# A cross-attention and maxout kernel: wider idle matmuls, two loads split in two, and a late copy of the states

## The chip, the cores and the metric

The kernel runs on one core of one Trainium2 chip. A core has five engines that run side by side, each through its own list of instructions in order: TensorE (PE in the profile, with its weight loads shown apart as PEld), VectorE (DVE), ScalarE (ACT), GpSimd (POOL) and SyncE (SP), which here issues nearly all the DMAs. An engine waits for another only through semaphores. TensorE writes to PSUM, whose banks hold 128 x 512 fp32 values; DVE and ACT copy from there to SBUF.

The metric is the device time of one execution in microseconds, and the number compared is the median over runs. Before the change it is 148.07 us, the median of 5 runs between 147.75 and 148.35.

## The reference, cut to what matters

```python
def _attn_ref(x, state):              # x: 8 x 8 x 512 x 64, state: 8 x 8 x 32 x 64
    scores = scale * x @ state.T;  a = softmax(scores);   xread = a @ state
    scores2 = scale * state @ x.T; a2 = softmax(scores2); sread = a2 @ x
    return concatenate([xread, sread], axis=2)

def _moe_ref(x, w1, w2, w_out):       # 4352 rows of 512 -> 1024 -> 512
    return np.maximum(x @ w1, x @ w2) @ w_out
```

For each batch and head, 512 rows of x read from 32 rows of state and the other way round. The result goes, token by token, through two matrices W1 and W2 of 512 x 1024, an elementwise maximum, and W_out (Wo in the code) of 1024 x 512.

## The kernel before

The kernel never forms `xread`. Since `xread = a @ state`, it multiplies the states of a batch into the weights first (`sw_mm`, tile `sw`) and then the attention weights `a` by that product. The maximum is rewritten: max(h1, h2) = h2 + relu(h1 - h2). So the first layer needs only W1 - W2 (tile `wd`, made by `w_sub`), followed by a relu into tile `r` (`l1_mm`, `l1_ev`), and the part h2 @ Wo becomes one product W2 @ Wo (tile `wwo`), made once from transposed W2 (`w2_tr_mm`, `w2t`) in `w_wo_mm`. The second layer adds up `a @ (state W2 Wo)` and `r @ Wo` in one PSUM bank for each of the four 128-row chunks of a batch (`l2_open`, `l2_f`, `l2_out`).

The order of all instructions is written out by hand. There are two parts. Lines 587 to 855 are the prologue: it loads batches 0 to 3, the states and the weights, the weights in four quarters, and interleaves the work of batch 0 with the making of `wd` and `wwo`, quarter by quarter, as they arrive. It ends with the first layer of batch 1. Lines 858 to 894 are a loop over the batches from 1 on: second layer of batch b, with the scores, the softmax and the `sw` product of batch b + 1 between its chunks. So the second layer of batch 1 (`b == 1`) is the first thing in the loop, and the scores of batch 2 come just ahead of it.

TensorE has its own fillers: `idle(n)` issues n matmuls of zeros, 256 columns wide, into a bank that nobody reads. There are 32 of them: 15 at the start, and groups of one, three and four between the first steps of batch 0.

The states. The block-diagonal tile `sbd` holds the transposed states of all batches; its zeros are written once. The states of batches 0 and 1 go through TensorE. Those of batches 2 to 7 are loaded together (`sfr`), cast on POOL (`sbr`), and transposed by one DMA into the tile `stt` (`states_dma`). `states_ev(1, "A")` and `states_ev(0, "V")` (lines 829 and 831) then copy one half each of `stt` into `sbd`, on ACT and on DVE. They stand ahead of the first relus of batch 1 in the lists of both engines. `scores_mm` (line 262) reads `sbd` for its batch, and so does `sw_mm`.

PSUM is two pools of four banks, `ps` and `pa`. The eight first-layer products of batch 1 alternate between them, and the two small transposes behind them, `sread_tr_mm(1, pa)` and `sread_tr_mm(0, pa)` (lines 846 and 850, L353 in the profile), take the `pa` banks that the relus of steps 6 and 5 on ACT have emptied.

The first attention weights. `norm_mul_pair(0, 2, "P")` and `norm_mul_pair(0, 3, "V")` (lines 668 and 669) multiply the exponentials by the reciprocal sums for head pairs 2 and 3 of batch 0, on POOL and DVE; `at_mm` transposes the result.

The DMAs of SP go out in the order of the code. There are eight completion semaphores for them, taken in turn, so that a DMA is issued only when the one eight places earlier has landed; besides, a load into a buffer waits until that buffer's last reader is done.

Of the kernel before, what the change touches and what calls it, by code (L numbers as in the profile page):

```python
# [8 lines left out]
F32 = mybir.dt.float32  # L9
# [6 lines left out]
def kernel(  # L16
# [9 lines left out]
    nc = tc.nc  # L26
    B, H, S, D = x.shape
    _, _, Ns, _ = state.shape
    L = S + Ns
    DM = H * D  # L30
    FF = moe_w1.shape[1]
    NC = S // 128
    NF = FF // 128
    NQ = 4
    FQ = FF // NQ
# [5 lines left out]
    stage = ctx.enter_context(tc.tile_pool(name="stage", bufs=1))  # L41
# [5 lines left out]
    pa = ctx.enter_context(tc.tile_pool(name="pa", bufs=4, space=bass.MemoryType.PSUM))  # L47
    ctx.enter_context(tc.manual_schedule())

    def bank(dtype=F32, pool=None):  # L50
        n = 512 if dtype == F32 else 1024
        if pool is pa:
            return pa.tile([128, n], dtype, tag="acc", name="acc")
        return ps.tile([128, n], dtype, tag="ps", name="ps")

    def copy(eng, o, i):
        if eng == "A":
            nc.scalar.copy(o, i)  # L58
        elif eng == "V":
            nc.vector.tensor_copy(o, i)  # L60
        else:
            nc.gpsimd.tensor_copy(o, i)  # L62
# [4 lines left out]
    wz = consts.tile([128, 512], BF16, name="wz")  # L67
    sbd = consts.tile([128, B, 4, 2 * Ns], BF16, name="sbd")
    wd = consts.tile([128, 4, FF], BF16, name="wd")
    wwo = consts.tile([128, 4, DM], BF16, name="wwo")  # L70
    wo = consts.tile([128, NF, DM], BF16, name="wo")
# [11 lines left out]
    xf_t, st = {}, {}  # L83
# [12 lines left out]
    w2f, w1f, wof, w2b = {}, {}, {}, {}  # L96

    def load_w2(q, second=False):
        wf, w, tag = (w1f, moe_w1, "w1f") if second else (w2f, moe_w2, "w2f")
        wf[q] = stage.tile([128, 4, FQ], F32, tag=tag, bufs=3, name=tag)  # L100
        nc.sync.dma_start(out=wf[q], in_=w[:, q * FQ:(q + 1) * FQ].rearrange("(i p) f -> p i f", p=128))

    def load_w1(q):
        load_w2(q, True)

    def load_wo(q):
        wof[q] = stage.tile([128, 2, DM], F32, tag="wof", bufs=3, name="wof")
        nc.sync.dma_start(out=wof[q], in_=moe_w_out[q * FQ:(q + 1) * FQ, :].rearrange("(f p) n -> p f n", p=128))  # L108
# [15 lines left out]
    P = {}  # L124
# [35 lines left out]
        P["st"] = xio.tile([128, NC * 256], BF16, tag="xb", name="stt")  # L160
        nc.sync.dma_start_transpose(out=P["st"].rearrange("p (m r) -> p m r", m=8), in_=sbr.rearrange("p m j d -> p (m j d)"))

    def states_ev(j, eng):
        o = sbd[64 * j:64 * j + 64, 2:B, :, 32 * j:32 * j + 32].rearrange("p b k (l m) -> p (b k) l m", l=4)
        copy(eng, o, P["st"][64 * j:64 * j + 64, :].rearrange("p (m k l) -> p k l m", m=8, l=4)[:, 8:])


    def cast_half(b, g, eng):
# [5 lines left out]
    def cast_x(b, engs):  # L174
        for g in range(2):
            cast_half(b, g, engs[g])
# [11 lines left out]
    def cast_pair(b, k, eng, m=1):  # L188
        xo = st[b]["xo"]
        for j in range(k, k + m):  # L190
            copy(eng, xo[:, :, j, 2:130].rearrange("p c (i d) -> p i c d", i=2),
                 xf_t[b][:, 2 * j:2 * j + 2, :].rearrange("p i (c d) -> p i c d", c=NC))

    def xt_pair_mm(b, k, pool=None):
        d = st[b]
        if "xt" not in d:
            d["xt"] = at.tile([128, NC, 4, 128], BF16, tag="xt", name="xt")
        p = P["xt", k] = bank(BF16, pool)
        for c in range(NC):
            nc.tensor.transpose(p[:, c * 128:(c + 1) * 128], d["xo"][:, c, k, 2:130], ident)  # L200

    def xt_pair_ev(b, k, eng):
        copy(eng, st[b]["xt"][:, :, k, :], P["xt", k][:, 0:512].rearrange("p (c t) -> p c t", c=NC))

    def att_tiles(b):
        d = st[b]
        d["e"] = at.tile([128, 2, NC, 4, Ns], BF16, tag="e", name="e")
        d["a"] = at.tile([128, 2, NC, 4, Ns], BF16, tag="a", name="a")
        d["es"] = at.tile([128, 2, 2 * NC, 2], F32, tag="es", name="es")
        d["er"] = at.tile([128, 2, 2 * NC, 2], F32, tag="er", name="er")  # L210

    def scores_pair_mm(b, k, pool):
        d = st[b]
        if "e" not in d:
            att_tiles(b)
        p = P["sc", k] = bank(F32, pool)
        for c in range(NC):
            nc.tensor.matmul(p[:, c * 64:c * 64 + 64], d["xt"][:, c, k, :], sbd[:, b, k, :],
                             start=(c == 0), stop=(c == NC - 1))
# [74 lines left out]
        (nc.gpsimd if eng == "P" else nc.vector).tensor_mul(  # L294
            av, ev, d["er"][:, hh].unsqueeze(3).to_broadcast([128, 2 * NC, 2, Ns]))

    def norm_mul_pair(b, k, eng):
        d = st[b]
        ev = d["e"].rearrange("p g c i n -> p (g c) i n")[:, :, k, :]
        av = d["a"].rearrange("p g c i n -> p (g c) i n")[:, :, k, :]  # L300
        (nc.gpsimd if eng == "P" else nc.vector).tensor_mul(
            av, ev, d["er"][:, k // 2, :, k % 2].unsqueeze(2).to_broadcast([128, 2 * NC, Ns]))

    def norm(b, hh, eng, sums=True):
        norm_sums(b, hh, sums)
# [137 lines left out]
    def l2_open(b, c, p, start, stop):  # L443
        for g in range(2):
            nc.tensor.matmul(p, AT[b][:, g, c, :], SW[b][:, g, FF:WC], start=(start and g == 0), stop=(stop and g == 1))  # L445

    def l2_f(b, c, p, fs, start, stop):
        for j, f in enumerate(fs):
            nc.tensor.matmul(p, R[b][:, f, c * 128:(c + 1) * 128], wo[:, f, :],  # L449
                             start=(start and j == 0), stop=(stop and j == len(fs) - 1))  # L450

    def l2_out(b, c, p, eng):
        if b not in OB:
            OB[b] = big.tile([128, NC, DM], F32, tag="ob", name="ob")
        copy(eng, OB[b][:, c, :], p)

    def l2(b, c):
        p = bank(F32, pa)
        l2_open(b, c, p, True, False)
        l2_f(b, c, p, range(NF), False, True)  # L460
        l2_out(b, c, p, "A" if c % 2 else "V")
# [56 lines left out]
    def w1_cast_h(j, eng):  # L518
        copy(eng, w1b[:, :, 128 * j:128 * j + 128], w1f[0][:, :, 128 * j:128 * j + 128])

    def wo_cast_h(j, eng):
        copy(eng, wo[:, j, :], wof[0][:, j, :])
# [23 lines left out]
    def w_sub(q, i0, i1, eng):  # L546
        (nc.gpsimd if eng == "P" else nc.vector).tensor_sub(  # L547
            wd[:, i0:i1, q * FQ:(q + 1) * FQ], w1f[q][:, i0:i1], w2f[q][:, i0:i1])

    def wo_cast(q, eng):  # L550
        copy(eng, wo[:, 2 * q:2 * q + 2, :], wof[q])

    ROUNDS = [[0], [1], [2], [3]]

    def w_wo_mm(r, i, pool=None):
        p = P["wwo", r, i] = bank(F32, pool)
        fs = [f for q in ROUNDS[r] for f in (2 * q, 2 * q + 1)]
        for f in fs:
# [7 lines left out]
    def w_wo_ev(r, i, eng):  # L566
        if r == 0:
            copy(eng, w2acc[:, i, :], P["wwo", r, i])
        else:
            nc.vector.tensor_tensor(wwo[:, i, :] if r == len(ROUNDS) - 1 else w2acc[:, i, :], P["wwo", r, i],  # L570
                                    w2acc[:, i, :], op=ALU.add)

    idle_p = [None]

    def idle(n, cols=256):
        if idle_p[0] is None:
            idle_p[0] = bank(F32, pa)
        for j in range(n):
            nc.tensor.matmul(idle_p[0][:, 0:cols], wz[:, 0:128], wz[:, 0:cols], start=True, stop=True)  # L579

    def l2_part(q, c):
        if ACC[c] is None:
# [14 lines left out]
    load_h(1, 0)  # L597
    load_state(1, nc.sync)
    load_w2(1)
    load_w1(1)  # L600
    load_wo(1)
    load_w2(2)
    load_w1(2)
    load_w2(3)
# [31 lines left out]
    scores_pair_mm(0, 0, pa)  # L636
    idle(1)
    cast_pair(0, 3, "V")
    xt_pair_mm(0, 2)
    xt_pair_ev(0, 2, "V")  # L640
    state0_neg("P")
    scores_pair_ev(0, 0)
    reduce_pair(0, 0)
    scores_pair_mm(0, 1, pa)
    scores_pair_ev(0, 1)
    reduce_pair(0, 1)
    w2_cast_h(0, "P")
# [17 lines left out]
    sw_h_mm(0, pa)  # L665
    reduce_pair(0, 3)
    norm_sums(0, 1, False)
    norm_mul_pair(0, 2, "P")
    norm_mul_pair(0, 3, "V")
    wo_cast_h(0, "P")  # L670
    w1_cast_h(1, "P")
    w2_tr_h_ev(0, "A")
# [38 lines left out]
    sw_ev(1, 0, FQ, 0, "A")  # L711
    l2_part(0, 0)
    w2_tr_mm(1)
    w_sub(1, 0, 4, "V")
    w2_tr_ev(1, "V")
    wo_cast(1, "P")
    sw_two_mm(1)
    sw_two_ev(1, 1, "V")
    w_wo_ev(0, 0, "A")
# [106 lines left out]
    l2_open(0, 0, ACC[0], False, True)  # L826
    l2_open(0, 1, ACC[1], False, True)
    l2_out(0, 1, ACC[1], "A")
    states_ev(1, "A")
    l2_out(0, 0, ACC[0], "V")  # L830
    states_ev(0, "V")
    l1_mm(1, 6, pa)
    cast_half(3, 1, "P")
    l1_ev(1, 6, "A")
# [23 lines left out]
    for b in range(1, B):  # L858
        n = b + 1
        if b + 2 < B:  # L860
            if b > 1:
                cast_x(b + 2, ("P", "P"))
                xt_dma(b + 2)
        for f in range(NF if b > 1 else 0):
            l1(b, f)
        if n < B:
            for hh in range(2):
                scores(n, hh)
            for hh in range(2):
                norm(n, hh, "P")  # L870
            at_dma(n)
            if b + 2 < B:
                cast_xo(b + 2)
            if b + 3 < B:
                load_x(b + 3)
        else:
            moe_sread()
        for c in range(NC):
            if b == B - 1 and c == NC - 1:
                l2_last(b, c)  # L880
            else:
                l2(b, c)
            if n < B:
                if c == 1:
                    sw_all(n)
                    sread_mm(n, pa)
                if c == 2:
                    sread_norm(n)
                if c == 3:
                    sread_tr(n, "A")  # L890
            elif c < NC - 1:
                store(b, c, c + 1)
        if n < B:
            store(b)
# [30 lines left out]
```

## Time and profile before

| | before |
|---|---|
| median of 5 runs | 148.07 us (147.75 to 148.35) |
| the profiled execution | 148.48 us, of which 146.7 us are the span that the trace covers |
| PE busy | 138.7 us (95% of the span) |
| DVE, ACT, POOL busy | 84.3, 70.0, 59.6 us |
| DMA | 29.44 MB, 15.34 MB read from and 8.91 MB written to HBM |
| granted TensorE clock | 1.00 in every stretch looked at |

The two times of the execution differ by 1.8 us, which lie around the span. The share of 95% for PE doesn't say that TensorE streams at its best all the time: the ends of matmuls are modelled, and one 128x512 matmul is shown with 0.38 us even where eight of them in a row start 0.216 us apart. So waits of TensorE are better read from start times than from the busy share.

DMA shares and rates by slice (each slice is 3.67 us):

```profile
DMA  4999999999939989487948684877307032402422
GB/s 135 314 324 353 355 362 363 361 349 170 177 77 358 136 280 306 92 195 291 262 91 289 243 192 76 282 290 147 72 0 288 7 72 107 179 4 72 143 111 103
```

Slices 4 to 9, from 11 to 33 us, move 349 to 363 GB/s without a gap: this is where weights, x of batches 1 to 3 and the states come in. Behind that the rate comes and goes with the loop.

### The profile page before, as it was taken

The page shows a single profiled execution, that of the slowest core. Times are in us where ns is not written, and L with a number is a line of the kernel's source. Part 1 is how long each engine was busy: PE and PEld are TensorE (multiplying, and loading weights), DVE is VectorE, ACT ScalarE, POOL GpSimd, SP SyncE. Part 2 cuts the span into 40 slices and gives each one's busy share as a digit, 9 for nine tenths or more (in the row PEclk, how much of TensorE's full clock was granted, in tenths as well). Part 3 has the DMA queues.
Part 4 walks back from the last instruction along what each step waited for, and adds up shares of the span by engine and source line. Part 5 has one row for each costly group of instructions (what it writes and reads, how often), then busy time and mean ns, then how long its engine had stood idle before and what let it go on. Part 6 is the DMA issues. An engine that isn't in the chain of part 4 may idle for free.

```text
span 146.7 us, 3194 instructions
## 1 busy us (share of the span) xinstructions
PE 138.7 (95%) x1281; PEld 69.8 (48%) x1300; DVE 84.3 (57%) x173; ACT 70.0 (48%) x135; POOL 59.6 (41%) x81
## 2 busy tenths in 40 slices
PE   6799999999979999999999999999999999999990
PEld 4465454364544445444544454454445444754460
DVE  3585695878866648464855585376547464621110
ACT  4377757686691546236541735171537145511110
POOL 2279635658936541925292448146600500000000
PEclk9999999999999999999999999999999999999999
DMA  4999999999939989487948684877307032402422
GB/s 135 314 324 353 355 362 363 361 349 170 177 77 358 136 280 306 92 195 291 262 91 289 243 192 76 282 290 147 72 0 288 7 72 107 179 4 72 143 111 103
DMA packets 37695, 29.44 MB, mean 201 GB/s; under 512 B 21296, under 2 KB 34864, under 8 KB 36784
## 3 DMA queue, kind: packets, MB, share of 16 engines
q1 hardware_dynamic: 37408, 29.17, 69.7%
q8 instruction: 10, 0.16, 0.5%
q10 hardware_dynamic: 272, 0.07, 0.2%
q14 instruction: 5, 0.04, 0.1%
HBM read 15.34 MB, written 8.91 MB: 165 GB/s over the span
## 4 chain that ended last, share of the span: by engine, by line
PE 69%; DMA 14%; SPq 6%; POOL 4%; ACT 3%; issue 1%; DVE 1%; POOLq 0%
PE acc L449 33%; PE ps L433 14%; DMA xf<-in_x_dram 9%; PE acc L445 7%; DMA stt<-sbr 5%; PE ps L489 2%; PE acc L499 2%; PE ps L368 2%; SPq L91 2%; PE ps L271 2%; SPq L149 2%; POOL wd L547 2%; PE acc L335 1%; SPq L108 1%; PE acc L473 1%
## 5 line engine op out<-in xcount | busy, mean ns | idle before, releaser
L449 PE MATMUL acc<-wo,r 128*128 128x512 bf16 x246 | 59.4, 380 | 0.4
L449 PEld LDWEIGHTS <-r 128*128 128x128 bf16 x248 | 23.8, 98 | 28.8 <-issue 0.6
L58 ACT COPY ob<-acc 128x512 f32<-128x512 f32 (+2 forms) x17 | 9.4, 554 | 49.1 <-PE acc L449 27.7
L433 PE MATMUL ps<-aT,sw 128*128 128x512 bf16 x117 | 27.7, 379 | 0.0
L424 DVE TENSOR_SCALAR r<-ps 128x512 bf16<-128x512 f32 x26 | 18.0, 691 | 14.3 <-PE ps L433 14.2
L294 POOL TENSOR_TENSOR a<-e,er 128x512 bf16<-128x512 bf16 x14 | 14.4, 1048 | 26.9 <-ACT e L276 19.1
L422 ACT ACTIVATE r<-ps 128x512 bf16<-128x512 f32 x33 | 19.5, 602 | 5.3 <-PE ps L433 4.7
L60 DVE COPY ob<-acc 128x512 f32<-128x512 f32 (+1 forms) x17 | 10.9, 644 | 16.4 <-PE acc L449 14.6
L62 POOL CAST xb<-xf 128x1024 bf16<-128x1024 f32 x12 | 13.5, 1128 | 15.9 <-DMA xf<-in_x_dram 15.9
L62 POOL CAST xo<-xf 128x512 bf16<-128x512 f32 x28 | 16.1, 615 | 6.7 <-DMA xf<-in_x_dram 6.3
L433 PEld LDWEIGHTS <-sw 128*128 128x128 bf16 x128 | 12.1, 98 | 13.7
L60 DVE CAST sw<-ps 128x512 bf16<-128x512 f32 x15 | 9.8, 686 | 11.0 <-PE ps L368 10.6
L445 PE MATMUL acc<-sw,aT 128*128 128x512 bf16 x49 | 15.6, 381 | 0.3
L58 ACT CAST sw<-ps 128x512 bf16<-128x512 f32 (+1 forms) x21 | 11.0, 573 | 2.7 <-PE ps L368 1.5
L287 DVE TENSOR_REDUCE es<-e 128x16 f32<-128x512 bf16 x14 | 9.2, 656 | 2.1 <-ACT e L276 2.1
L276 ACT ACTIVATE e<-ps 128x512 bf16<-128x512 f32 x14 | 7.8, 604 | 0.8 <-PE ps L271 0.2
L579 PE MATMUL acc<-wz 128*128 128x256 bf16 x32 | 6.7, 347 | 1.2 <-DVE ones L617 1.2
L445 PEld LDWEIGHTS <-aT 128*128 128x128 bf16 x62 | 5.0, 98 | 4.4
L559 PE MATMUL ps<-wo,w2t 128*128 128x512 bf16 x23 | 6.5, 380 | 0.2
L570 DVE TENSOR_TENSOR w2acc<-ps,w2acc 128x512 f32<-128x512 f32 x8 | 5.2, 686 | 1.7 <-PE ps L559 1.5
L271 PEld LDWEIGHTS <-xt 128*128 128x128 bf16 x112 | 4.3, 98 | 2.5 <-issue 0.9
L547 POOL TENSOR_TENSOR wd<-w1f,w2f 128x1024 bf16<-128x1024 f32 x2 | 4.7, 2355 | 1.7 <-DMA w1f<-in_moe_w_dram 1.7
(109 smaller groups left out, 145.0 us busy)
## 6 DMA issues: line engine op xcount, KB each, us to landing
xf<-in_x_dram SPq DMA_DIRECT2D x14, 512.0 KB, 5.1
out_dram<-ob SPq DMA_DIRECT2D x7, 1024.0 KB, 4.2
w2f<-in_moe_w_dram SPq DMA_DIRECT2D x3, 512.0 KB, 6.5
w1f<-in_moe_w_dram SPq DMA_DIRECT2D x3, 512.0 KB, 8.4
wof<-in_moe_w_out_dram SPq DMA_DIRECT2D x3, 512.0 KB, 7.9
xf<-in_x_dram SPq DMA_DIRECT2D x4, 256.0 KB, 3.9
out_dram<-ob SPq DMA_DIRECT2D x3, 256.0 KB, 2.0
w2f<-in_moe_w_dram SPq DMA_DIRECT2D x2, 256.0 KB, 5.8
```

The costliest lines, as they stand in the source:

```text
L58: nc.scalar.copy(o, i)
L60: nc.vector.tensor_copy(o, i)
L62: nc.gpsimd.tensor_copy(o, i)
L276: nc.scalar.activation(out=ev.rearrange("p (g c) i n -> p g c (i n)", g=2), in_=P["sc", hh].rearrange("p (c g m) -> p g c m", c=NC, g=2), ...
L287: nc.vector.tensor_reduce(d["es"][:, hh], ev, axis=mybir.AxisListType.X, op=ALU.add)
L294: (nc.gpsimd if eng == "P" else nc.vector).tensor_mul(av, ev, d["er"][:, hh].unsqueeze(3).to_broadcast([128, 2 * NC, 2, Ns]))
L422: nc.scalar.activation(out=o, in_=p, func=ACTF.Relu)
L424: nc.vector.tensor_scalar(o, p, scalar1=0.0, scalar2=None, op0=ALU.max)
L433: nc.tensor.matmul(p, SW[b][:, g, f * 128:(f + 1) * 128], AT[b][:, g].rearrange("p c t -> p (c t)"), start=(g == 0), stop=(g == 1))
L445: nc.tensor.matmul(p, AT[b][:, g, c, :], SW[b][:, g, FF:WC], start=(start and g == 0), stop=(stop and g == 1))
L449: nc.tensor.matmul(p, R[b][:, f, c * 128:(c + 1) * 128], wo[:, f, :], start=(start and j == 0), stop=(stop and j == len(fs) - 1))
L547: (nc.gpsimd if eng == "P" else nc.vector).tensor_sub(wd[:, i0:i1, q * FQ:(q + 1) * FQ], w1f[q][:, i0:i1], w2f[q][:, i0:i1])
```

## The change

Seven edits go together:

- `idle(n)` issues half as many matmuls of twice the width (512 columns), and one of 256 columns more where n is odd. 32 instructions become 20, with the same number of columns.
- The load of the second quarter of W1 is issued in two halves by rows, and that of Wo in two halves by rows: four DMAs of 256 KB in place of two of 512 KB.
- `w_sub(1, ...)` on DVE becomes two instructions, one for each half of W1; the cast of Wo's second quarter on POOL becomes two.
- `norm_mul_pair(0, 2)` is cut by chunk group: half stays on POOL, half goes to DVE behind `norm_mul_pair(0, 3)`.
- `scores_pair_mm(0, 1)` moves ahead of `xt_pair_mm(0, 2)` on TensorE.
- `states_ev` takes a range of batches. Where it stood, it copies batch 2 alone (of six batches).
- The copies for batches 3 to 7 follow the first chunk of batch 1's second layer in the loop.

```diff
+    def load_w1_part(q, g):
+        if q not in w1f:
+            w1f[q] = stage.tile([128, 4, FQ], F32, tag="w1f", bufs=3, name="w1f")
+        nc.sync.dma_start(
+            out=w1f[q][:, 2 * g:2 * g + 2],
+            in_=moe_w1[256 * g:256 * g + 256, q * FQ:(q + 1) * FQ].rearrange("(i p) f -> p i f", p=128))
+
+    def load_wo_part(q, j):
+        if q not in wof:
+            wof[q] = stage.tile([128, 2, DM], F32, tag="wof", bufs=3, name="wof")
+        nc.sync.dma_start(out=wof[q][:, j, :], in_=moe_w_out[q * FQ + 128 * j:q * FQ + 128 * j + 128, :])
...
-    def states_ev(j, eng):
-        o = sbd[64 * j:64 * j + 64, 2:B, :, 32 * j:32 * j + 32].rearrange("p b k (l m) -> p (b k) l m", l=4)
-        copy(eng, o, P["st"][64 * j:64 * j + 64, :].rearrange("p (m k l) -> p k l m", m=8, l=4)[:, 8:])
+    def states_ev(j, b0, b1, eng):
+        o = sbd[64 * j:64 * j + 64, b0:b1, :, 32 * j:32 * j + 32].rearrange("p b k (l m) -> p (b k) l m", l=4)
+        copy(eng, o, P["st"][64 * j:64 * j + 64, :].rearrange("p (m k l) -> p k l m", m=8, l=4)[:, 4 * b0:4 * b1])
...
-    def norm_mul_pair(b, k, eng):
+    def norm_mul_pair(b, k, eng, g0=0, g1=2):
         d = st[b]
-        ev = d["e"].rearrange("p g c i n -> p (g c) i n")[:, :, k, :]
-        av = d["a"].rearrange("p g c i n -> p (g c) i n")[:, :, k, :]
+        gs = slice(NC * g0, NC * g1)
+        ev = d["e"].rearrange("p g c i n -> p (g c) i n")[:, gs, k, :]
+        av = d["a"].rearrange("p g c i n -> p (g c) i n")[:, gs, k, :]
         (nc.gpsimd if eng == "P" else nc.vector).tensor_mul(
-            av, ev, d["er"][:, k // 2, :, k % 2].unsqueeze(2).to_broadcast([128, 2 * NC, Ns]))
+            av, ev, d["er"][:, k // 2, gs, k % 2].unsqueeze(2).to_broadcast([128, NC * (g1 - g0), Ns]))
...
+    def wo_cast_part(q, j, eng):
+        copy(eng, wo[:, 2 * q + j, :], wof[q][:, j, :])
...
-        for j in range(n):
-            nc.tensor.matmul(idle_p[0][:, 0:cols], wz[:, 0:128], wz[:, 0:cols], start=True, stop=True)
+        for w in [2 * cols] * (n // 2) + [cols] * (n % 2):
+            nc.tensor.matmul(idle_p[0][:, 0:w], wz[:, 0:128], wz[:, 0:w], start=True, stop=True)
...
-    load_w1(1)
-    load_wo(1)
+    load_w1_part(1, 0)
+    load_w1_part(1, 1)
+    load_wo_part(1, 0)
+    load_wo_part(1, 1)
...
     cast_pair(0, 3, "V")
+    scores_pair_mm(0, 1, pa)
     xt_pair_mm(0, 2)
     xt_pair_ev(0, 2, "V")
     state0_neg("P")
     scores_pair_ev(0, 0)
     reduce_pair(0, 0)
-    scores_pair_mm(0, 1, pa)
...
-    norm_mul_pair(0, 2, "P")
+    norm_mul_pair(0, 2, "P", 0, 1)
     norm_mul_pair(0, 3, "V")
+    norm_mul_pair(0, 2, "V", 1, 2)
...
-    w_sub(1, 0, 4, "V")
+    w_sub(1, 0, 2, "V")
+    w_sub(1, 2, 4, "V")
     w2_tr_ev(1, "V")
-    wo_cast(1, "P")
+    wo_cast_part(1, 0, "P")
+    wo_cast_part(1, 1, "P")
...
-    states_ev(1, "A")
+    states_ev(1, 2, 3, "A")
     l2_out(0, 0, ACC[0], "V")
-    states_ev(0, "V")
+    states_ev(0, 2, 3, "V")
...
             else:
                 l2(b, c)
+            if b == 1 and c == 0:
+                states_ev(1, 3, B, "A")
+                states_ev(0, 3, B, "V")
```

## The prediction

> **What bounds the kernel now.** I read the windows first, then TensorE's own list where the windows show a hole, then the chain of waits for who made the hole. The windows give busy time by engine for a stretch (start:end, length, PE, PEld, DVE, ACT, POOL, clock, DMA share, GB/s):
>
> ```profile
> 40.00:43.50 3.50, 2.65 (x27) 1.39 (x26) 2.81 (x6) 3.48 (x7) 1.57 (x1) 1.00 0.38 78
> 43.50:57.35 13.85, 13.71 (x127) 6.48 (x129) 8.18 (x17) 6.47 (x14) 6.57 (x9) 1.00 0.96 275
> 57.35:71.20 13.85, 13.75 (x128) 6.47 (x129) 8.21 (x18) 6.17 (x13) 6.56 (x9) 1.00 0.78 210
> ```
>
> From 43.5 us on, a batch takes 13.85 us and TensorE is busy for all of it: nothing can be won there but by fewer columns. From 40 to 43.5 us it idles 0.85 us by this modelled count (3.50 - 2.65), while ACT is full (3.48 of 3.5). TensorE's list there shows the hole by start times:
>
> ```profile
> 40.94 0.59 PE L433 MATMUL ps<-aT,sw 128*128 128x512 bf16 x2
> 41.61 0.22 PE L353 MATMUL acc<-ident,sr 128*128 128x128 bf16 x1
> 42.59 0.21 PE L353 MATMUL acc<-ident,sr 128*128 128x128 bf16 x1 [0.76 <-ACT r L422]
> 42.65 0.63 PE L271 MATMUL ps<-sbd,xt 128*128 128x64 bf16 x16
> 43.11 0.38 PE L445 MATMUL acc<-sw,aT 128*128 128x512 bf16 x1
> ```
>
> A 128x512 matmul in a row takes 0.216 us (eight in 1.73 us in the chain), so the first-layer stream of batch 1 ends at 40.94 + 2 x 0.216 = 41.37. The first L353 starts at 41.61 (0.24 late), streams some 0.06, and the second waits from 41.67 to 42.59 (0.92). Together **1.16 us** in which TensorE had nothing else in its list. The chain of waits names the cause (start, length, what):
>
> ```profile
> 32.12 7.28 DMA stt<-sbr
> 39.40 0.02 issue
> 39.42 1.52 ACT sbd L58
> 40.95 0.02 issue
> 40.96 1.58 ACT r L422 x3
> 42.55 0.04 issue
> 42.59 0.21 PE acc L353
> ```
>
> The transposed states land at 39.40; ACT copies all six batches of them for 1.52 us before the first relu of batch 1, and the third relu frees the bank that the second L353 waits for.
>
> Before 40 us TensorE is full as well. Counting start times with 0.216 us for 512 columns, the real waits after 12.3 us are one at 15.85 (0.2, for `sbd` on DVE) and one at 18.35 (0.3, for `w2t` and `wo`). So a delay put in at 12 us comes out at the end unabsorbed, while a gain lasts only until TensorE meets the next load.
>
> **The states' copies** (the main term). The rows of the tile `sbd` (line, engine, operation, count: shortest/median/longest ns, first and last start, shape):
>
> ```profile
> L58 ACT COPY sbd<-ps x2: 258/260/261, 4.7 to 5.0; 64x128 bf16<-64x128 bf16 x2
> L60 DVE COPY sbd<-ps x2: 282/288/295, 15.2 to 15.5; 64x128 bf16<-64x128 bf16 x2
> ...
> L58 ACT COPY sbd<-stt x1: 1516/1516/1516, 39.4 to 39.4; 64x768 bf16<-64x768 bf16 x1
> L60 DVE COPY sbd<-stt x1: 1240/1240/1240, 39.4 to 39.4; 64x768 bf16<-64x768 bf16 x1
> ```
>
> Batch 2 alone is 64x128: 0.26 us on ACT, 0.29 on DVE. The remaining 64x640, by the line through both sizes: (1516 - 260)/640 = 1.96 ns per element, so 1.27 us on ACT; 1.05 us on DVE.
>
> ACT's new order: copy 39.42 to 39.68, then five relus 0.49 us apart (they start at 40.96, 41.46, 41.93 before). The relus of steps 6, 4, 5 end at about 40.3, 40.8, 41.3, so both banks are free when the stream ends at 41.37. Step 7 ends at 41.75, step 2, whose product is done at about 41.55, at 42.25. DVE does its three relus between 39.8 and 42.0. Next: is something else late? The scores of batch 2 need `xt`, which was issued at 36.54 and took 4.4 us, so 40.94: in time. The scores then run from 41.5, the second layer opens at about 41.95 instead of 43.11, and its first L449 starts at 42.4 instead of 43.54; the last relu is needed two matmuls later, at 42.8, and is there at 42.25. **The whole 1.16 us goes.** Both ends: all of it, or, if relus and evictions come half a microsecond later than this, about 0.7.
>
> What the moved copies cost: ACT has 3.13 us idle ahead of its next eviction (47.63), where 1.27 us find room; its two exponentials come first in its list, so what feeds the softmax isn't delayed. DVE has 1.53 us idle between the eviction of chunk 0 (ends 46.46) and the `sw` evictions at 47.99, where 1.05 fit with 0.5 to spare. The scores of batch 3, which need them, come 10 us later. I take nothing.
>
> Here a rule speaks against the change. The Trainium skill, "SBUF — State Buffer", section "Who interferes with whom", says that a DVE copy in a two-port mode and a GpSimd instruction lock each other out for a whole instruction. The moved DVE copy would now fall beside POOL's normalisation of batch 2 (44.1 to 46.2) or its casts. The nearest row agrees in kind:
>
> ```profile
> 38.95 2.62 POOL L62 CAST xb<-xf 128x1024 bf16<-128x1024 f32 x2
> ...
> 52.96 1.04 POOL L62 CAST xb<-xf 128x1024 bf16<-128x1024 f32 x1 [3.18 <-DMA xf<-in_x_dram]
> ```
>
> Beside the old DVE copy two casts took 2.62 us, where one takes 1.04 elsewhere: 0.54 lost. By the row `at_dma(2)` would be issued 0.5 later, by the rule 1.05. It was issued at 47.31 and took 4.0 us, so 51.3, for the first layer of batch 2 at 53.04: 1.7 us of slack. By either, the sum gets nothing.
>
> **The early edits.** The rows, from the timeline:
>
> ```profile
> 1.19 3.38 PE L579 MATMUL acc<-wz 128*128 128x256 bf16 x15 [1.19 <-DVE ones L617]
> ...
> 10.34 0.79 POOL L301 TENSOR_TENSOR a<-e,er 128x256 bf16<-128x256 bf16 x1 [0.26 <-DVE er L288]
> ...
> 17.21 1.04 POOL L62 CAST wo<-wof 128x1024 bf16<-128x1024 f32 x1 [1.11 <-DMA wof<-in_moe_w_out_dram]
> ```
>
> Idle matmuls: the columns stay. Fifteen of 256 take 3.38 us; with some 0.39 for the last, that is 0.213 from start to start, just their columns at the half rate of the start, so the weight loads are hidden already, and seven of 512 with one of 256 take the same 3.4 us. Nothing (a gain of 0.05 at most; a loss only by the clock, under the rivals).
>
> `scores_pair_mm(0, 1)` was held behind transposes that wait for a POOL cast until 7.03; ahead of them it can run at about 6.1. Its exponential ran at 7.58, but DVE reduces only at 7.87, right behind its own copy. Nothing.
>
> The halved multiplication: POOL takes 1.05 us for 512 elements and 0.79 for 256, so for 128 between 0.40 (proportional) and 0.66 (by the line); I take 0.6. DVE's half (some 0.3) ends at about 10.95. The transposes at 11.19 waited for POOL until 11.13; TensorE itself comes free at 11.0. So 0.13 to 0.2 us here, and about as much at 12.29, where `w1b` from POOL was awaited.
>
> The split loads: a half lands 0.72 us before the whole (512 KB land 1.45 us apart: 13.7, 15.85, 17.16, 18.7 for the second quarter and on). The first half of Wo can be cast before 17.16, so POOL ends at about 17.8 and not 18.25, and the wait at 18.35 can follow the earlier TensorE. `w_sub` starts behind the `sbd` copies at 15.79, with whole W1 in at 15.85: worth 0.06. A rule against it: the skill's "DMA: Bandwidth & Descriptors", "Rules for kernel authors", says to put small transfers together, with a fixed cost of some 2 us each ("Anatomy of one DMA", fitted for another issuing engine). By the rule, estimate, two more transfers would be up to 4 us of DMA time. But six 256 KB loads landed at 7.9, 8.8, 9.4, 10.4, 11.3 and 12.1: 0.84 us each, with the fixed part overlapped. So at most 0.1 us per extra DMA; I take 0. On SP two more issues of 0.5 us, and the turn of semaphores moves W2 and W1 of the third quarter behind landings at 11.3 and 12.1 (before: 10.07 and 10.58). Some 1.8 MB are then still outstanding, 5 us of work, and the next load waits for POOL until 15.13 anyway. Hidden; if it weren't, each microsecond would show whole.
>
> **How much of that lasts?** TensorE may come up to 0.3 us early to 18.4, but at 30.40 a weight load waited for ACT's cast of x of batch 1, which waited for its load (29.6), and the L244 at 30.55 followed 0.15 later. Loads land at the full rate, so they don't move. I keep **0.05** (0 to 0.15).
>
> Sum: 148.48 - 1.16 - 0.05 = 147.27 for the profiled execution, which lies 0.41 above the median of runs; taken to the median, 148.07 - 1.2 = **146.9 us**.
>
> **Rivals.**
>
> - The moved copy becomes a new wait: if POOL holds it up or it takes 2 us on DVE, the `sw` evictions of batch 2 come some 0.6 us late, and banks are short. 147.5. For: only 0.5 us to spare. Against: ACT takes half of those evictions and has more room.
> - The early gain lasts: if x of batch 1 lands earlier too, 0.3 us more: 146.5. Against: the full DMA rate.
> - The stall stays because something else is late by as much (the transposed `xt`, PSUM banks): 148.1, as if nothing had been done. For: `xt` has only 0.6 us to spare.
> - Slower, by the clock. At 4.46 four transposes took 0.64, at 5.16 only 0.41: TensorE's clock rises near 5 us. The skill's "TensorE: Matmul & The Clock Gate", Part 1, has it granted after a busy window of some 3.4 us. Should wide zeros count for less activity and the rise come one window late (8.6), the chain of batch 0 loses about 0.4 (transposes and scores at half rate, mostly beside waits for loads): 147.3. Two windows late (12.0), TensorE's full stretch from 8.6 loses some 2.5 more: 149.8. It decides from about 9.5 us on. Against: the same columns, back to back.
>
> **Chances.** Forecast 0.62, new wait 0.12, early gain lasting 0.12, stall stays 0.07, slower 0.07. A change below 0.3%, 0.44 us, can't be told from none. Most of the second rival is still faster: faster 0.81, same 0.12, slower 0.07. The range, 146.3 to 147.9, takes in the first three and the ends of the main term.
>
> **What would show it.** L353 twice within 0.1 us right behind the last L433; first L449 of batch 1 at 42.3 to 42.5; `sbd<-stt` on ACT at 0.26 us; a loop of 13.85 us per batch as before; L244 still near 30.5. Wrong it would be if TensorE waits at L271, at L368 near 46.4, or if the first L200 transposes all take 0.64.

## The result, and the profile after

| | before | after |
|---|---|---|
| median of the runs taken side by side | 148.31 us (79 runs) | 147.66 us (44 runs) |
| ratio, 95% interval | | 0.9956 [0.9941, 0.997] |
| the profiled execution | 148.48 us, span 146.7 | 148.52 us, span 146.7 |

The kernel is faster by 0.65 us. The sign is the forecast's and the time lies in its range, but the gain is about half of the 1.2 us that the sum gave. About one execution in five of either kernel (53 of 258 of before, 13 of 66 of after, by their mean granted clock) has TensorE's clock halved for 3.4 us near 8 us, which costs some 1 us; where that would hide a difference I also give the mean of the executions whose mean granted clock is at least 0.995.

The two profiled executions are equally long, so one might read from them that nothing was gained. The timeline of the changed kernel (start, busy time, engine, line, operation; the old L353, L271, L445, L449, L433 are now L367, L284, L459, L463, L447) shows otherwise:

```profile
40.09 0.41 ACT L58 COPY sbd<-stt 64x128 bf16<-64x128 bf16 x1
...
42.30 0.60 PE L447 MATMUL ps<-aT,sw 128*128 128x512 bf16 x2
...
42.73 0.28 PE L367 MATMUL acc<-ident,sr 128*128 128x128 bf16 x2
...
42.84 0.63 PE L284 MATMUL ps<-sbd,xt 128*128 128x64 bf16 x16
...
43.31 0.60 PE L459 MATMUL acc<-sw,aT 128*128 128x512 bf16 x2
...
43.74 1.89 PE L463 MATMUL acc<-wo,r 128*128 128x512 bf16 x8
```

The stream ends at 42.30 + 2 x 0.216 = 42.73, and both small transposes start there and then, one row with x2 where there were two rows 0.98 apart. The stall of 1.16 us is gone. The windows say the same (columns as in the prediction's: PE now fills the 3.70 us to the end, and a batch still takes 13.85):

```profile
40.00:43.70 3.70, 3.70 (x34) 1.97 (x33) 3.61 (x8) 3.31 (x8) 2.37 (x3) 1.00 0.51 98
43.70:57.55 13.85, 13.69 (x127) 6.48 (x129) 9.59 (x18) 7.57 (x14) 6.82 (x9) 1.00 1.01 284
```

From the first L244 (now L257) to the first L449 of batch 1, before's profile needs 13.86 us (29.68 to 43.54) and after's 12.71 (31.03 to 43.74): 1.16 less. What ate it in this execution came earlier. TensorE reached L257 1.36 us later, because its clock rose late. Its list (PE only) shows four transposes at 0.61 still at 7.98, a duration that before's profile had left behind at 5.16 (0.41):

```profile
7.98 0.61 PE L213 MATMUL ps<-ident,xo 128*128 128x128 bf16 x4
...
10.51 0.31 PE L596 MATMUL acc<-wz 128*128 128x256 bf16 x1 [0.22 <-issue]
...
12.23 0.61 PE L338 MATMUL ps<-ident,a 128*128 128x128 bf16 x8
```

L338 (the old L324) starts at 12.23 where it was 11.19. Whether the change causes this is a question for the experiments. They find no cost of it in the time (e2, e3); whether the wide idle matmuls can delay the rise stays open (last section).

The copies themselves, from the rows of the tile `stt` (shortest/median/longest ns, first and last start, shapes):

```profile
L58 ACT COPY sbd<-stt x2: 411/850/1288, 40.1 to 44.5; 64x128 bf16<-64x128 bf16 x1, 64x640 bf16<-64x640 bf16 x1
...
L60 DVE COPY sbd<-stt x2: 720/1108/1497, 40.7 to 46.4; 64x128 bf16<-64x128 bf16 x1, 64x640 bf16<-64x640 bf16 x1
```

### The profile page after: what moved, and what is told of

It is laid out like the page before. It is cut to its first block, busy times and chain, and to the rows that moved or that the text cites. A ratio compares the mean times of both kernels' runs of the same rounds, so it can differ in the third digit from the quotient of the medians.

```text
span 146.7 us, 3176 instructions
## 1 busy us (share of the span) xinstructions
PE 139.7 (95%) x1267; PEld 69.7 (48%) x1288; DVE 86.5 (59%) x176; ACT 70.2 (48%) x136; POOL 60.2 (41%) x82
## 4 chain that ended last, share of the span: by engine, by line
PE 90%; DMA 3%; DVE 2%; issue 1%; SPq 1%; POOL 0%; ACT 0%; POOLq 0%
PE acc L463 36%; PE ps L447 17%; PE acc L459 9%; PE ps L576 3%; DMA xf<-in_x_dram 3%; PE ps L382 3%; PE ps L503 2%; PE acc L513 2%; PE ps L284 2%; PE acc L349 2%; PE acc L596 1%; DVE wd L561 1%; PE acc L447 1%; PE acc L487 1%; PE acc L511 1%
## 5 line engine op out<-in xcount | busy, mean ns | idle before, releaser
L463 PE MATMUL acc<-wo,r 128*128 128x512 bf16 x243 | 58.7, 380 | 0.8 <-issue 0.3
L463 PEld LDWEIGHTS <-r 128*128 128x128 bf16 x248 | 23.7, 98 | 28.8 <-issue 0.6
L447 PE MATMUL ps<-aT,sw 128*128 128x512 bf16 x118 | 27.9, 380 | 0.0
L62 POOL CAST xb<-xf 128x1024 bf16<-128x1024 f32 x12 | 12.9, 1082 | 20.0 <-DMA xf<-in_x_dram 20.0
L447 PEld LDWEIGHTS <-sw 128*128 128x128 bf16 x128 | 12.1, 98 | 13.7
L459 PE MATMUL acc<-sw,aT 128*128 128x512 bf16 x50 | 15.6, 381 | 0.3
L596 PE MATMUL acc<-wz 128*128 128x512 bf16 (+1 forms) x18 | 7.1, 494 | 1.6 <-DVE ones L636 1.2
L459 PEld LDWEIGHTS <-aT 128*128 128x128 bf16 x62 | 5.0, 98 | 4.4
L62 POOL CAST w2b<-w2f 128x1024 bf16<-128x1024 f32 (+1 forms) x4 | 4.3, 1083 | 2.8 <-DMA w2f<-in_moe_w_dram 2.7
```

Of the source, the lines that this page charges most:

```text
L447: nc.tensor.matmul(p, SW[b][:, g, f * 128:(f + 1) * 128], AT[b][:, g].rearrange("p c t -> p (c t)"), start=(g == 0), stop=(g == 1))
L596: nc.tensor.matmul(idle_p[0][:, 0:w], wz[:, 0:128], wz[:, 0:w], start=True, stop=True)
```

## The experiments

My theory at first: the stall is gone wherever the states are copied late, and where the time doesn't show it, the clock hides it. The rivals: the wide idle matmuls delay the clock; the split subtraction costs what the late copy brings; or the stall depends on something that only some executions have.

**One part alone (e1, e2), one part undone (e3, e4).** e1 is before with the split `states_ev` and its late call, and nothing else; e2 is before with the new `idle`; e3 is after with the old one; e4 is after with one `w_sub` in place of two:

```diff
# e2 (e3 is the reverse, on after)
-        for j in range(n):
-            nc.tensor.matmul(idle_p[0][:, 0:cols], wz[:, 0:128], wz[:, 0:cols], start=True, stop=True)
+        for w in [2 * cols] * (n // 2) + [cols] * (n % 2):
+            nc.tensor.matmul(idle_p[0][:, 0:w], wz[:, 0:128], wz[:, 0:w], start=True, stop=True)
# e4
-    w_sub(1, 0, 2, "V")
-    w_sub(1, 2, 4, "V")
+    w_sub(1, 0, 4, "V")
```

> The kernel before with the late copy of the states alone. All theories: the 1.16 us stall at L353 goes and nothing else changes, so 1.1 us below before, ratio 0.992 to 0.993; in the profile the first L449 of batch 1 stands about 1.1 us closer to the first L244 than before. If it gives only 0.6 us, the stall was mis-sized and the other edits are innocent.

> The kernel before with the wide idle matmuls alone. Theory C (wide zeros delay the rise of TensorE's clock, 10.6 us in the profile of after against 5.2 in that of before): 0.4 to 0.9 us slower, ratio 1.003 to 1.006, and a rise near 10 us in its profile. Theory P (the rise falls where a free-running window happens to stand, in both kernels alike): the same time, ratio 0.999 to 1.001.

> The changed kernel with the idle matmuls of before (256 columns, 32 of them). Theory C: 0.4 to 0.9 us below the changed kernel, ratio to before 0.990 to 0.993. Theory P: as the changed kernel, ratio to before 0.9955.

> The changed kernel with the subtraction of the second quarter in one DVE instruction again (the loads stay in halves). Theory W (the two halves, 2.16 us together in the profile of after against 1.24 for the whole, run beside POOL's casts and make TensorE wait 0.4 us for wd): about 0.4 us below the changed kernel, ratio to before 0.992 to 0.993. Theory C: as the changed kernel, 0.9955.

Measured: e1 0.9951 [0.9925, 0.9976], e2 0.9989 [0.9967, 1.001], e3 0.9936 [0.9916, 0.9955], e4 0.994 [0.9917, 0.9962]. The late copy alone gives what the whole change gives, 0.60 us. The wide idle matmuls alone change nothing, and undoing them or the halved subtraction gives nothing that can be told from the whole change. e3's profile, with the old idle matmuls, also had a bad clock (it rose early, but was halved from 8.0 to 11.4), so a slow clock in this stretch doesn't need the wide ones. But the size was a puzzle: 0.60 us, where a stall of 1.16 is gone in all three profiles that have the late copy.

**TensorE late on purpose (e5, e6).** Ten more 128x512 matmuls ahead of step 6 of batch 1, into the bank that step 6's real product then overwrites, in both kernels (e5 before, e6 after):

```diff
         p = P["l1", f] = bank(F32, pool)
+        for _ in range(10 if (b, f) == (1, 6) else 0):
+            nc.tensor.matmul(p, SW[b][:, 0, f * 128:(f + 1) * 128], AT[b][:, 0].rearrange("p c t -> p (c t)"), start=True, stop=True)
```

> The kernel before with ten more 128x512 matmuls (2.16 us of TensorE's stream, into a bank that the real product then overwrites) right ahead of the first layer of batch 1. Theory A (the stall at L353 is a wait for the transposed states, which land at a time set by the DMAs; a TensorE that is late spends less of it): the stall is used up, so the cost is 2.16 less the stall that runs have on average, some 0.6: 1.5 us, ratio 1.010; no gap at L353 in its profile. Rival F (every run has the 1.16 us stall, and the change lost half of its gain elsewhere): 1.0 us, ratio 1.007.

> The changed kernel with the same ten matmuls at the same place. No stall is left to use up: 2.16 us more than the changed kernel, so by theory A ratio to before 0.9956 + 0.0146 = 1.010, the same as the kernel before with the ten; by rival F also 1.010, but 0.5 us above the kernel before with the ten.

e5 1.0086 [1.0049, 1.0123], e6 1.0072 [1.005, 1.0093]. The stretch from L244 to L449 is 14.862 us in e5 and 14.866 in e6. That closes the account: before's 13.864 + 10 x 0.216 - 1.16 = 14.86, after's 12.707 + 2.16 = 14.87. With TensorE 2.16 us later the old order has no stall either, and the late copy shortens nothing. So the stall is a date of ACT against a date of TensorE. The ten matmuls move only the second: they stand behind the product whose eviction ACT's copy follows.

**Fillers where the clock is at risk (e7, e8).** Four more idle matmuls near 7 us, in after ahead of `xt_pair_mm(0, 2)` and in before at the `idle(1)` above it:

```diff
# e7, on after
     scores_pair_mm(0, 1, pa)
+    idle(4)
     xt_pair_mm(0, 2)
# e8, on before
     scores_pair_mm(0, 0, pa)
-    idle(1)
+    idle(5)
     cast_pair(0, 3, "V")
```

> The changed kernel with four more idle matmuls of 256 columns' worth (two of 512) where TensorE waits for the third cast of x, between about 6.1 and 7.0 us. If the late rises and drops of TensorE's clock come from windows that this wait leaves too idle, the slow end of the runs (148 us and more) goes: median 0.2 to 0.5 us below the changed kernel, ratio to before 0.992 to 0.994, and a rise before 8 us in its profile with no drop behind it. If the rise is set by the window's place alone: as the changed kernel, 0.9955.

> The kernel before with four more idle matmuls at the same wait. If early lateness of TensorE is partly absorbed by the later stall (theory A), the fill brings less here than in the changed kernel: 0 to 0.2 us, ratio 0.9985 to 1.000; by rival F as much as there.

e7 0.9952 [0.9934, 0.997], e8 0.9978 [0.9959, 0.9997]. The fillers do what they are for: none of the 44 timed executions (22 each) had the halved clock, against 13 of 59 of before beside them. But a wait that strikes one execution in five moves a median little. Two things came out of the profiles. In e8 the stall was not 1.16 but 0.51. And in e7 a new wait stands where the stall was (timeline and the weight loads of the scores):

```profile
41.88 0.28 PE L367 MATMUL acc<-ident,sr 128*128 128x128 bf16 x2
...
42.68 0.52 PEld L284 LDWEIGHTS <-xt 128*128 128x128 bf16 x16 [0.70 <-DMA xt<-xb]
```

The transposed `xt` of batch 2 landed 5.6 us after its issue here, and not 4.4, so the scores waited 0.7 us. That is the prediction's third rival, the slack of 0.6 us on `xt`, at work in one execution.

**Is the stall the landing of the states? (e9, e10).** The loads of batch 3's x go behind `states_dma` instead of ahead of the first steps (e9 before, e10 after), so that the states land early:

```diff
     states_dma()
+    load_x(3, 2, 0)
+    load_x(3, 2, 1)
```

> The kernel before with the load of x of batch 3 issued behind the transpose of the states and not ahead of it, nothing else: 1 MB, some 2.9 us of DMA time, then lies behind the states in the queue. If the stall is a wait for the states' landing (theory A), the states land 2 to 3 us earlier against the other loads, the six-batch copies are done before TensorE needs the banks, and the stall goes without any of the edits: gap at L353 below 0.2 us in the profile, and the same gain as the change has, ratio 0.994 to 0.997. If the stall is ACT's own load (the copies ahead of five relus, whenever the states land): the gap stays at 0.5 or more and the ratio is 0.999 to 1.001.

> The changed kernel with the same move of the load of x of batch 3. Nothing is left to win at L353; the wait for the transposed x of batch 2 that one profile showed behind it (0.69 us) stays or goes with the transposes' place in the queue: by theory A 0 to 0.2 us below the changed kernel, ratio 0.994 to 0.996. If the two gains were independent: 0.991.

e9 1.0001 [0.997, 1.0031], e10 0.9974 [0.9957, 0.9992]. In e9 the states land 3.5 us after issue instead of 7.3 (tile `stt`), at 35.3, and ACT's copy doesn't start before 39.88:

```profile
L58 ACT COPY sbd<-stt x1: 1552/1552/1552, 39.9 to 39.9; 64x768 bf16<-64x768 bf16 x1
...
DMA to landing us min/median/max: 3.5/3.5/3.5
```

Its L353 stand at 42.52 and 43.09, a stall of 0.51. So the theory that the stall is a wait for the landing falls: with the states there 4.6 us early, half a microsecond stays. It is ACT's own list, where the copy follows an eviction and takes 1.55 us ahead of five relus. e10 lost part of its gain to `xt`, which landed after 5.8 us, behind batch 3's x (0.9 us of wait at the scores).

**The early edits alone (e11, e15), and the same with the late copy (e14).** e11 is after with the six-batch copies where they stood. e14 is after with the old idle matmuls and one `w_sub`; e15 is e14 with the six-batch copies:

```diff
# e11, and e15 on e14
-    states_ev(1, 2, 3, "A")
+    states_ev(1, "A")
...
-    states_ev(0, 2, 3, "V")
+    states_ev(0, "V")
...
-            if b == 1 and c == 0:
-                states_ev(1, 3, B, "A")
-                states_ev(0, 3, B, "V")
```

> The changed kernel with the copies of the states as before (all six batches, ahead of the relus): the early edits alone. Theory A: what they save early is spent at the stall: 0 to 0.1 us, ratio 0.999 to 1.000. If they save or cost by themselves (split subtraction, split loads): outside 0.997 to 1.002.

> The changed kernel with idle matmuls of 256 columns and the subtraction in one instruction again; split loads, split cast, halved multiplication, the moved scores and the late copy of the states stay. Neither of the two taken back showed an effect of its own, so as the best of the others: ratio 0.993 to 0.996. If the split subtraction or the wide matmuls cost something after all: 0.991 to 0.993.

> The same as e14 with the six-batch copies of the states where they stood before, on the same chip beside it: the worth of the late copy alone. Theory B: 0.5 to 0.7 us slower than e14, less what a wait for the transposed x of batch 2 takes from e14: 0.3 to 0.7, and a stall of 0.5 or more at L353 in this one's profile. If the early edits make the late copy worthless (each alone gave the gain of both): within 0.1 us of e14.

e11 0.9953 [0.993, 0.9976], e14 0.9952 [0.9926, 0.9978], e15 0.9998 [0.9973, 1.0022]. Side by side on one chip, the late copy is worth 148.08 - 147.47 = 0.61 us (e15, e14), and the early edits left in e15 nothing that can be told. But e11, in an earlier set of runs on the same chip, had nearly the whole gain without the late copy. e11 and e15 differ by idle width and `w_sub` alone, for which e2, e3 and e4 had found nothing.

**Before again (e12, e13).** Only for the profile: is 1.16 us what this kernel does?

> The kernel before once more, for its profile. Theory B (of the stall at L353 only 0.51 us belongs to ACT's list, whenever the states land; the rest, up to 0.65, is a wait for their landing that not every execution has): a stall of 0.5 where the transpose of the states lands 5.8 us after its issue, up to 1.2 where it takes 7.3. Theory of the prediction: 1.16 again.

> The kernel before a third time, as e12: by theory B 0.5 or, with a landing of 7.3 us, up to 1.2; by the prediction 1.16.

It isn't. e12 (151.07 us, with a halved clock from 8.7 to 12.1) had a stall of 0.50, e13 (148.46 us) one of 0.86. The timeline of e13:

```profile
39.38 1.54 ACT L58 COPY sbd<-stt 64x768 bf16<-64x768 bf16 x1 [0.40 <-DMA stt<-sbr]
...
41.64 0.22 PE L353 MATMUL acc<-ident,sr 128*128 128x128 bf16 x1
...
42.56 0.22 PE L353 MATMUL acc<-ident,sr 128*128 128x128 bf16 x1 [0.70 <-ACT r L422]
```

**All four corners on one chip (e16, e17, e18):** after, e11's kernel and e1's kernel again.

> The changed kernel beside the two kernels that have only one side of the change, on one chip. Theory A (the late copy is worth some 0.6 us by itself, the early edits nothing that can be told): ratio near 0.9955, 0.6 to 0.7 us below the kernel before, and no stall at the two small transposes. Theory B (each side of the change is worth some 0.6 us and the two do not add, because what one gains the other has no room for): the same 0.9955, so this run serves as the yardstick for the next two.

> The early edits alone: the changed kernel with the six-batch copies where they stood. Theory A: 0.998 to 1.001 and 0.4 to 0.6 us more than the changed kernel; the profile shows the stall of at least 0.5 us. Theory B: 0.9955, within 0.2 us of the changed kernel, as the earlier run of it (0.9953) had it.

> The late copy alone, all early edits as before. Theory A: 0.9955, within 0.2 us of the changed kernel. Theory B: also 0.9955; the two part at the early edits alone. If the late copy alone came out near 1.000 here, the first run of it would have been scatter and theory A falls.

e16 0.9951 [0.9926, 0.9975], e17 0.9945 [0.9923, 0.9966], e18 0.9959 [0.9936, 0.9982]. Theory A, which gave the early edits nothing, fails for this kernel: in e11 and e17 they are as good alone as the whole change. Over the executions whose mean clock is at least 0.995, from all chips, the means with their 95% bounds are

| | executions | mean us |
|---|---|---|
| before | 205 | 148.31 ± 0.06 |
| late copy alone (e1, e18) | 33 | 147.73 ± 0.13 |
| early edits alone (e11, e17) | 33 | 147.67 ± 0.13 |
| both (after, e16) | 53 | 147.57 ± 0.13 |
| early edits, but old idle matmuls and one `w_sub` (e15) | 16 | 148.00 ± 0.14 |
| the same with the late copy (e14) | 16 | 147.32 ± 0.19 |

By the first four rows each half is worth about 0.6 us and both together 0.74, so they would share a gain. The last two speak against that: there the early edits give 0.31 (0.19 against the executions of before beside them), and the late copy 0.68 on top. So the late copy alone is worth about 0.6 us, twice; what the early edits are worth, 0.2 to 0.6, stays open. e17's profile shows what is left of the stall when only the early edits are in:

```profile
38.78 1.55 ACT L58 COPY sbd<-stt 64x768 bf16<-64x768 bf16 x1
...
41.43 0.22 PE L367 MATMUL acc<-ident,sr 128*128 128x128 bf16 x1
...
41.99 0.22 PE L367 MATMUL acc<-ident,sr 128*128 128x128 bf16 x1 [0.34 <-ACT r L436]
```

ACT doesn't wait for the states any more (no bracket behind its copy), and the stall is 0.51.

**What the profiles say together.** In the nine profiles with the six-batch copy and no matmuls added right ahead of the stall, with D the copy's start less the end of the stream: D = -1.95 in before's profile, stall 1.16; -2.27, 0.86 (e13); -2.47, 0.67 (e15); -2.63 to -2.65, 0.50 to 0.51 (e2, e8, e9, e11, e12, e17). The stall is D + 3.12 in all of them, within 0.03. ACT's own list sets the floor of 0.5; above it the states' landing decides. Their transposing DMA lands 7.2 to 7.3 us after its issue in e1, e8, e13, e15, e18 and before's profile, 5.8 to 5.9 us in e2, e12 and in all nine profiles of after and its variants with split loads other than e10 and e15 (e5: 6.8). So with the early edits the landing mostly comes before ACT wants it.

The packets in the traces narrow down what makes it 5.8 or 7.3. The states are 1024 packets of 256 bytes. From the start of the last of them to the landing it is 0.5 to 0.8 us in fourteen profiles, and 2.0 to 2.1 in the six with 7.2 to 7.3: the delay lies behind the transfer. In all six, SP's instruction for the next transposing DMA, `xt`, had started before that last packet (by 0.09 to 0.80 us). It had done so (by 0.06 us or more) in four that landed on time, all with split loads, and in none of the other ten. So an early `xt` is a candidate for the late landing. That it is the cause, and that the split loads help against it, is only argued from these counts. The time doesn't confirm the landing's part either: e9, where it is gone for certain, was no faster than before (1.0001, known to 0.3%).

One more part of the early edits' gain was in no sum. From the first L449 of batch 1 to the end of the span, all profiles with before's loads take 103.14 to 103.16 us, all with the split loads 103.00 to 103.02. The difference lies behind the last matmul: SP's last wait, for the output DMAs (count, longest: twice in before, once in after).

```profile
SPq L920 <- DMA out_dram<-ob: 1.4, 2, 1.2
```

```profile
SPq L945 <- DMA out_dram<-ob: 1.2, 1, 1.2
```

That is 0.14 us at the end of the program from edits at its start. Two more DMAs turn the eight completion semaphores by two places, which could do it, but that was not tried apart. e14 and e15 exclude the idle width and the halved subtraction.

Open: by the stall, the two halves together should give about 0.5 us more than the early edits alone, since that stall is 0.51 in both profiles and 0 with the late copy. By the medians e14 against e15 shows 0.61, e16 against e17 only 0.10. The new wait for `xt` (0.7 and 0.9 in e7 and e10) is a candidate for what is given back, but it stood in no profile of after itself.

No version was clearly better than the changed kernel; e3, at 0.9936, overlaps it.

## Why the prediction was right in kind and wrong in size

**The step that failed is "The whole 1.16 us goes. Both ends: all of it, or, if relus and evictions come half a microsecond later than this, about 0.7."** The mechanism holds in every profile with the late copy: L353 twice within 0.06 us right behind the stream, in ACT's order as foretold. The size is wrong because 1.16 is the stall of one execution. 0.51 of it is ACT's list; 0.65 is a wait for a landing, which other executions of the same kernel have at 0.35 (e13) or not at all (e12). The mean over the nine profiles is 0.64, and the late copy alone measured 0.60 (e1) and 0.57 (e18), below the low end of 0.7. The row was there: ACT's copy had 0.72 us of idle ahead of it, put down to the DMA. At ACT's own date, 39.42 - 0.72 = 38.70, D is -2.67 and the stall 0.45. The low end should have been that, and the sum "taken to the median" should have asked whether the 0.41 us by which the profiled execution lay above the median sat in this very wait. That the time still fell in the range is no merit of the sum: the range was wide, and the early edits and the end of the program gave something that the sum had at 0.05.

**Moved copies at nothing: right, with wrong sizes.** The small copies take 0.41 us on ACT (0.26 estimated) and 0.72 on DVE (0.29), the large ones 1.29 (1.27) and 1.50 on DVE (1.05). On ACT `sbd<-ps` was a poor row for `sbd<-stt`, which reads another layout, from SBUF. On DVE it was a good one, as e10 shows, where POOL stands idle beside the small copy:

```profile
L60 DVE COPY sbd<-stt x2: 253/855/1457, 39.4 to 45.8; 64x128 bf16<-64x128 bf16 x1, 64x640 bf16<-64x640 bf16 x1
```

In the nine other profiles with the late copy a POOL cast is running when DVE starts, and DVE's copy ends 0.11 to 0.12 us after that cast. So the lock between DVE and POOL, which the prediction looked for only at the large copy, is real here and takes 0.47 us of DVE's time. It costs TensorE nothing: all copies fit in the idle time, as the loop of 13.85 shows, so the first rival (a new wait at the `sw` evictions) didn't come.

**Early edits at 0.05: the path as described, the sum too small.** TensorE's gain does end at x of batch 1: in profiles whose clock rose by 6.0 us and stayed, with nothing added ahead of it, L244 stands at 29.41 to 29.95 without the early edits and at 29.38 to 29.89 with them. Yet alone they measured 0.2 to 0.6 us. The profiles account for about 0.3: 0.14 at the end of the program, and some 0.15 of stall (mean 0.71 in the five profiles with before's loads in their place, 0.56 in e11, e15 and e17). The rest is open. No step of the sum followed the two added DMAs that far: it went "past" SP's queue only up to the third quarter's weights. (The four landings quoted for "1.45 us apart" lie 2.1, 1.3 and 1.5 apart; the halves did land 0.7 apart in after's profile.)

**Idle matmuls at nothing: right** in the time (e2). **The halved subtraction, "worth 0.06":** beside POOL's casts of Wo its halves took 2.16 us together in after's profile, against 1.24 for the whole before; e4 shows no difference in time.

**Rivals.** The slower one by the clock: the late rise exists, in after's own profile, and its cost (L338 at 12.23 there, at 10.78 to 11.36 in e4, e11, e14, e15, e17, which have an early rise) lies between the two cases put down, 0.4 and 2.9 us. How often it comes isn't known: the mean granted clock doesn't count the time ahead of the first rise (it is 1.000 in that profile). What it does count, a drop behind an early rise, strikes both kernels alike, in 53 of 258 executions before and 13 of 66 after. "Stall stays because `xt` is late" happened in part, in e7 and e10.

**"A delay put in at 12 us comes out at the end unabsorbed": wrong here.** With a late TensorE the landing's part of the stall is gone (e2, e12), and a delay of 2.16 us put in behind ACT's eviction takes all of it (e5).

## What to carry to other kernels

A stall is a difference between two dates, and one profile gives it once: split it into what the waiting engine's own list makes and what a landing makes, and count only the first as sure. Two edits that both shorten the same wait need not add, so test each alone and both on one chip. Follow added DMAs to the end of the program, not only past the next few loads.

## What the hardware showed that I had not expected

**The clock near the start.** In the 20 profiles the granted clock rose between 4.3 and 6.6 us, once at 10.6, and moved in steps of 3.41 us. (The Trainium skill, "TensorE: Matmul & The Clock Gate", Part 1, has a free-running window of 3413 ns; the steps agree.) Whether it stays goes with how busy TensorE is in the window behind the rise. Two windows each of e13 and e12, before's kernel both times (PE's busy time is the first number behind the length, the granted clock the third from the end):

```profile
5.77:9.18 3.41, 2.04 (x32) 1.30 (x30) 2.25 (x6) 1.57 (x4) 2.12 (x3) 1.00 1.13 327
9.18:12.59 3.41, 3.38 (x83) 2.01 (x81) 1.94 (x5) 2.94 (x8) 3.02 (x5) 1.00 1.12 327
```

```profile
5.31:8.72 3.41, 1.82 (x29) 1.28 (x29) 1.95 (x6) 0.80 (x3) 1.68 (x3) 1.00 1.09 334
8.72:12.13 3.41, 3.41 (x62) 2.05 (x67) 2.22 (x7) 2.22 (x5) 2.48 (x4) 0.50 1.12 318
```

With 2.04 us busy of 3.41 the next window has full clock, with 1.82 half. Over all 20 profiles this busy time separates without exception: 2.04 to 3.25 us in the 15 that kept the clock, 1.35 to 1.98 in the five that lost it for one window. The hole is the wait for the first x (e16: 1.35 us ahead of the transposes at 7.66), so it depends on when a load lands; with fillers in it, the drop was gone from all 44 executions of e7 and e8. Executions of before with such a mean clock average 149.40 us against 148.31.

One thing speaks for the rival that the wide idle matmuls delay the rise: all five rises later than 5.8 us (5.94, 5.99, 6.25, 6.62 and 10.59) are among the nine profiles that have them, and none is among the eleven with the narrow ones. It was not followed up; the time of e2 shows no cost.

**A transposing DMA of the same bytes** took 5.8 or 7.3 us to land, once 6.8, and 3.2 to 3.5 without batch 3's x ahead of it (e9, e10); that of `xt` took 4.2 to 4.9, or 5.6 and 5.8 (e7, e10).

**A DVE copy beside a POOL cast** took 0.72 to 0.74 us, where the same copy took 0.25 with POOL idle.
